# Chunked attention and two gated layers on one core: attention on 64x32 and 64x64 tiles of TensorE

## The chip, the cores and the metric

The kernel runs on one core of a Trainium2 chip. The metric is the device time of one execution in microseconds. A profile shows, for one execution, every instruction of the core's engines: TensorE (PE for its matmuls, PEld for its weight loads), VectorE (DVE), ScalarE (ACT), GpSimd (POOL), and SyncE (SP), which issues the DMA transfers.

## The reference

The program is an attention over chunks, followed by two feed-forward layers on its output. All is in float32.

```python
def _attn_ref(q, k, v, mem_k, mem_v):        # q, k, v: 4 x 8 x 768 x 64, mem: 8 rows
    chunk, left_ctx, right_ctx = (32, 16, 8)
    for c in range(nc):
        k_full = concat(mem_k, k[l_start:r_end]); v_full = concat(mem_v, v[l_start:r_end])
        scores = scale * q_c @ k_full.T
        scores = scores - max(scores, axis=-1)
        a = exp(scores); a = a / (sum(a, axis=-1) + 1e-09)
        out[c_start:c_end] = a @ v_full

def _moe_ref(x, w_in, w_out, alpha):         # 3072 x 512, d_ff = 2048
    h = x @ w_in
    return (maximum(h, 0) + alpha * minimum(h, 0)) @ w_out

def _moe2_ref(x, w_in, w_out):
    h = x @ w_in
    return (h * tanh(softplus(h))) @ w_out

x = attn_out as (3072, 512);  x = _moe_ref(x, ...);  return _moe2_ref(x, ...)
```

Each chunk has 32 queries and sees at most 16 + 32 + 8 keys and 8 memory rows, so 64 keys (the constant SW).

## The kernel before, in words

The weights come as 64-bit words and are turned into float32 on the core (`to_f32`), then split in two parts, high and low (`split_w`), and so are the activations. A product of the feed-forward layers is three matmuls of 128x128 weights and 512 columns (high by high, high by low, low by high): line 694 for the first product of a layer (`gemm1`), line 758 for the second (`gemm2`). They run over 6 blocks of 512 tokens and 16 slices `j` of d_ff, in each of the two layers.

The attention works on 24 tiles of 128 tokens (4 blocks of batch and 6 tiles each). A tile T goes through these steps, and each of the first, third and fourth is a burst on TensorE:

- **scores** (`scores_of`, line 470): 16 matmuls, each with 128 rows of contraction and 64 columns of weights. Two heads share a matmul: the queries stand in a block-diagonal buffer `qbd`, of which half is zeros, so that 128 rows hold two heads of 64.
- **softmax**: on VectorE the maximum (line 485) and, at the end, the division (line 504); on ScalarE eight exponentials with their sums (line 488). Tile 3 takes another way, with one exponential.
- **turn**: the probabilities are transposed, for T < UPT = 5 by TensorE (`turn_pe`, line 580, 16 transposes of 64x96, then copies by `copy_on`, line 250), from then on by VectorE (`turn_dve`, line 606, 8 transposes of 32x256).
- **values** (`values_of`, line 537): 16 matmuls with 96 rows of contraction and 64 columns of weights. The result is split into the halves `xh` (line 554) and `xl` (line 558) of the layers' input.

A matmul of float32 is two passes, so 16 matmuls show 32 records of weight loads (LDWEIGHTS) and 32 of matmuls.

The tiles 0 to 3 (one block of 512 tokens, T < T0) are worked through in front of the layers. While TensorE would wait there, it runs matmuls on a buffer of zeros (`plan.fill`, line 820, called fills below); they stand in its order of work like any other instruction. The tiles 4 to 23 are woven into layer 1: `block_steps` lists the steps, and a step "sv" is one burst with the scores of tile T + 1 and the values of tile T. There are 19 such bursts; beside them stand the scores of tile 4, its transposes, and the values of tile 23, each in a burst of its own.

A planner (`Plan`) sets the order of the instructions on each engine from durations and dependences that the code gives it; the engines then wait on semaphores. PSUM has 8 banks of 512 float32 per partition; in the later part bank 6 takes the scores and bank 7 the values.

Of the kernel before, what the change touches and what calls it, by code (L numbers as in the profile page):

```python
# [174 lines left out]
def chunked_attention_moe_moe_kernel(  # L175
# [37 lines left out]
    UPT = 5  # L213
    BOTH = ("act", "dve")
    WHOLE = (3,)
    T0 = BLOCKS[0][1] // P

# [147 lines left out]
    vring = ring(ac, [W, 2 * DM], F32, "vw", 1)  # L365
# [4 lines left out]
    s_bufs = [own([P, 1024], "s"), spare_slot()]  # L370
    a_bufs = [own([W, 1024], "aT"), spare_slot()]

    def wide_of(b):
        return b.t.rearrange("p (g w) -> p g w", w=P)

    for b in s_bufs:
        for cols in (slice(0, CH), slice(CH + SW, P)):
            add("pool", 0.6, lambda b=b, cols=cols: nc.gpsimd.memset(wide_of(b)[:, :, cols], 0.0), writes=[b])
    for b in qbd:
        for h in range(2):  # L380
            add(
                "pool", 0.6,
                lambda b=b, h=h: nc.gpsimd.memset(
                    b.t.rearrange("p (g h x) -> p g h x", g=2 * NP, h=2)[(1 - h) * 64 : (2 - h) * 64, :, h], 0.0
                ),
                writes=[(b, 2 + h)],
            )
# [4 lines left out]
    att_bufs = [*s_bufs[:1], *a_bufs[:1], *qbd[:2]]  # L392
    n_ps = [0]

    def att_bank(T, late):
        n_ps[0] += 1
        return bank((0, 1, 2, 4, 5, 6, 7)[n_ps[0] % 7] if T < T0 else late)

    def load_qk(T):
        b, t = divmod(T, TPB)  # L400
        kt = kv_spare[T][0] if T in kv_spare else kring.next()
        qt = qbd[T if T < T0 else T % 2]

        def kview():
            return kt.t[:, : NP * KC].rearrange("p (a c) -> p a c", a=NP)

        def qview():
            return qt.t.rearrange("p (a e h x) -> p a e h x", a=NP, e=2, h=2)

        add("sp", dma_(P * NP * KC * 4), lambda: nc.sync.dma_start(kview(), kw[b, t]), writes=[kt])  # L410
        if T < T0:

            row = q_rows[T // 2], T % 2

            def rows():
                return row[0].t[:, row[1] * 512 : (row[1] + 1) * 512]

            add("sp", dma_(P * 2048), lambda: nc.sync.dma_start(rows(), q[b, t].rearrange("h d a e x -> (h d) (a e x)")), writes=[row])
            for h in range(2):

                def place(eng, h=h):
                    half = slice(h * 64, (h + 1) * 64)
                    copy_on(eng, qview()[half, :, :, h], rows()[half].rearrange("p (a e x) -> p a e x", a=NP, e=2))

                add(BOTH if T == 0 else "dve", 0.55, place if T == 0 else partial(place, "dve"), [row], [(qt, h)])
        else:
            for h in range(2):
                add(
                    "sp", dma_(P * 2048),
                    lambda h=h: nc.sync.dma_start(qview()[h * 64 : (h + 1) * 64, :, :, h], q[b, t, h]),  # L430
                    writes=[(qt, h)],
                )
        kts[T], qs[T] = (kt, kview), (qt, qview)
        att_bufs.append(kt)

    def load_v(T):
# [3 lines left out]
        def view():  # L440
            return v.t[:W].rearrange("w (e x) -> w e x", e=2)
# [3 lines left out]
        vws[T] = v, lambda: v.t[:W].rearrange("w (e h d) -> w e h d", e=2, h=H)  # L445
        att_bufs.append(v)

    def scores_of(T):

        t = T % TPB  # L450
        (kt, kview), (qt, qview) = kts[T], qs[T]
        bk = att_bank(T, 6)
        sb = s_bufs[T % 2 if T < T0 else 0]

        def s():
            return wide_of(sb)[:, :, CH : CH + SW]

        st = stats.next()
        ss[T] = sb

        def ps():
            return bk.t.rearrange("p (g c) -> p g c", c=SW)


        def go():
            for e in range(2):
                for p in range(NP):
                    for c in range(2):
                        k0 = e * (U + NM) + c * CH
                        nc.tensor.matmul(  # L470
                            ps()[c * 64 : (c + 1) * 64, e * NP + p, :],
                            qview()[:, p, e].rearrange("p h (x c) -> p (h x) c", c=2)[:, :, c],
                            kview()[:, p, k0 : k0 + SW],
                            start=True, stop=True,
                        )


        def clip():
            if t == 0:
                nc.vector.memset(ps()[0:64, 0:NP, 0:16], NEG)  # L480
            if t == TPB - 1:
                nc.vector.memset(ps()[64:128, NP:, SW - 8 :], NEG)

        def top():
            nc.vector.tensor_reduce(st.t[:, 0, :], ps(), AX.X, ALU.max, negate=True)

        def exps(g):
            nc.scalar.activation(
                s()[:, g, :], ps()[:, g, :], AF.Exp, bias=st.t[:, 0, g : g + 1], scale=0.125,
# [4 lines left out]
        def less():  # L494
            nc.vector.tensor_add(s(), ps(), st.t[:, 0, :].unsqueeze(2).broadcast_to([P, 2 * NP, SW]))  # L495

        def exp():
            nc.scalar.activation(s(), s(), AF.Exp, scale=0.125)
# [7 lines left out]
        def rest():  # L506
            if t in (0, TPB - 1):
                add("dve", 0.15, clip, [], [bk])
            add("dve", d_(512), top, [bk], [(st, 0)])
            if T in WHOLE:  # L510
                add("dve", d_(512), less, [(st, 0), bk], [sb])
                add("act", a_(512), exp, [], [sb])
                add("dve", d_(512), total, [sb], [(st, 1)])
            else:
                add("dve", 0.12, lambda: nc.vector.tensor_scalar_mul(st.t[:, 0, :], st.t[:, 0, :], 0.125), [], [(st, 0)])
                for g in range(2 * NP):
                    add("act", 0.29, lambda g=g: exps(g), [(st, 0), bk], [(sb, g), (st, 1, g)])
# [5 lines left out]
        return go, [kt, qt], [bk], rest  # L523

    def values_of(T):

        (ab, aT), (vb, v) = aTs.pop(T), vws.pop(T)
        bk = att_bank(T, 7)

        def ps():  # L530
            return bk.t.rearrange("p (a e c) -> p a e c", a=NP, e=2)

        def go():
            for e in range(2):
                for p in range(NP):
                    for h in range(2):
                        nc.tensor.matmul(  # L537
                            ps()[h * 64 : (h + 1) * 64, p, e].rearrange("d (c q) -> d c q", c=2),
                            v()[:, e, 2 * p + h, :], aT()[:, e * NP + p, h],
                            start=True, stop=True,  # L540
                        )

        def rest():
# [6 lines left out]
            def flat():  # L550
                return bk.t.rearrange("p (a n) -> p a n", a=NP)

            def high():
                nc.scalar.copy(views()[0][:, :, cols], flat())

            def low():
                xh, xl = (z[:, :, cols] for z in views())
                nc.vector.tensor_sub(xl, flat(), xh.bitcast(F32))
# [381 lines left out]
```

## Time and profile before

| what | us |
|---|---|
| median of 3 runs (1126.13 to 1127.2) | 1126.44 |
| the profiled execution | 1125.74 |
| its span, first to last instruction | 1123.6 |
| TensorE busy (99%) | 1116.2 |
| VectorE busy (71%) | 796.4 |
| ScalarE busy (52%) | 583.3 |

The profiled execution is 0.7 us below the median. A span is cut into stretches below by the start times of instructions; a matmul's record lasts from its issue to its modelled end, so records of matmuls that run behind one another overlap, and it is the distance of their starts that counts. The duration of a pass of 512 columns is 0.39 us, the distance of two of them 0.23 us.

### The profile page before, as it was taken

The page shows a single profiled execution, that of the slowest core. Times are in us where ns is not written, and L with a number is a line of the kernel's source. Part 1 is how long each engine was busy: PE and PEld are TensorE (multiplying, and loading weights), DVE is VectorE, ACT ScalarE, POOL GpSimd, SP SyncE. Part 2 cuts the span into 40 slices and gives each one's busy share as a digit, 9 for nine tenths or more (in the row PEclk, how much of TensorE's full clock was granted, in tenths as well). Part 3 has the DMA queues.
Part 4 walks back from the last instruction along what each step waited for, and adds up shares of the span by engine and source line. Part 5 has one row for each costly group of instructions (what it writes and reads, how often), then busy time and mean ns, then how long its engine had stood idle before and what let it go on. Part 6 is the DMA issues. An engine that isn't in the chain of part 4 may idle for free.

```text
span 1123.6 us, 16499 instructions
## 1 busy us (share of the span) xinstructions
PE 1116.2 (99%) x6286; PEld 920.4 (82%) x6291; DVE 796.4 (71%) x1402; ACT 583.3 (52%) x1268; POOL 6.6 (1%) x20
## 2 busy tenths in 40 slices
PE   8999999999999999999999999999999999999998
PEld 6888888888888888888888888888888888888886
DVE  6899844566556656635449788778878778777775
ACT  6876634454455445445456455445446445444543
POOL 2000000000000000000000000000000000000000
PEclk9999999999999999999999999999999999999999
DMA  9957212264453544334332002002002000100101
GB/s 281 286 172 216 74 37 70 69 181 125 138 157 109 166 124 149 99 104 139 94 101 96 1 1 75 1 1 75 1 1 71 6 1 19 38 1 1 38 1 38
DMA packets 71454, 94.26 MB, mean 84 GB/s; under 512 B 25296, under 2 KB 41680, under 8 KB 71376
## 3 DMA queue, kind: packets, MB, share of 16 engines
q1 hardware_dynamic: 71376, 93.22, 27.8%
q8 instruction: 49, 0.80, 0.3%
q14 instruction: 29, 0.24, 0.1%
HBM read 72.23 MB, written 20.97 MB: 83 GB/s over the span
## 4 chain that ended last, share of the span: by engine, by line
PE 99%; issue 0%; DVE 0%; ACT 0%
PE bank L694 47%; PE bank L758 47%; PE bank L470 2%; PE bank L537 2%; PE bank L820 1%; PE bank L580 0%; DVE wo L495 0%; ACT o L250 0%; DVE busy L818 0%; DVE wi L250 0%
## 5 line engine op out<-in xcount | busy, mean ns | idle before, releaser
L694 PE MATMUL bank<-xh,wi 128*128 128x512 f32 (+1 forms) x1552 | 507.0, 388 | 0.0
L694 PEld LDWEIGHTS bank<-xh,wi 128*128 128x128 f32 x1552 | 290.5, 188 | 60.4 <-DVE wi L332 0.2
L694 PE MATMUL bank<-xl,wi 128*128 128x512 f32 (+1 forms) x776 | 300.2, 387 | 0.0
L758 PE MATMUL bank<-gh,wo 128*128 128x512 f32 x768 | 253.3, 391 | 0.0
L758 PE MATMUL bank<-wo,gh 128*128 128x512 f32 x768 | 236.4, 389 | 0.0
L694 PEld LDWEIGHTS bank<-xl,wi 128*128 128x128 f32 x776 | 145.6, 188 | 29.2
L758 PEld LDWEIGHTS bank<-gh,wo 128*128 128x128 f32 x768 | 144.1, 188 | 30.6 <-DVE rstrip L250 0.3
L758 PEld LDWEIGHTS bank<-wo,gh 128*128 128x128 f32 x768 | 144.2, 188 | 29.9
L716 DVE SCALAR_TENSOR_TENSOR rstrip<-rstrip,nalpha 128x512 f32<-128x512 f32 x96 | 72.0, 750 | 113.8 <-ACT rstrip L713 113.2
L758 PE MATMUL bank<-gl,wo 128*128 128x512 f32 x384 | 149.4, 389 | 0.0
L758 PE MATMUL bank<-wo,gl 128*128 128x512 f32 x384 | 149.4, 389 | 0.0
L706 ACT CAST gh<-u 128x512 fp32r<-128x512 f32 x96 | 59.9, 624 | 156.4 <-PE bank L758 156.3
L712 ACT ACTIVATE rstrip<-bank 128x512 f32<-128x512 f32 x96 | 57.8, 602 | 123.2 <-PE bank L694 115.9
L707 DVE TENSOR_TENSOR gl<-rstrip,gh 128x512 fp32r<-128x512 f32 x96 | 66.3, 691 | 64.8 <-ACT gh L706 63.9
L725 ACT ACTIVATE u<-bank 128x512 f32<-128x512 f32 x96 | 57.5, 599 | 93.2 <-PE bank L694 92.5
L706 ACT CAST gh<-rstrip 128x512 fp32r<-128x512 f32 x96 | 60.1, 626 | 79.5 <-PE bank L758 65.5
L730 DVE SCALAR_TENSOR_TENSOR e<-n,rc 128x512 f32<-128x512 f32 x96 | 66.5, 692 | 48.6 <-ACT rc L729 48.6
L707 DVE TENSOR_TENSOR gl<-u,gh 128x512 fp32r<-128x512 f32 x96 | 66.4, 691 | 42.2 <-ACT gh L706 42.2
L758 PEld LDWEIGHTS bank<-wo,gl 128*128 128x128 f32 x384 | 72.0, 188 | 14.9
L758 PEld LDWEIGHTS bank<-gl,wo 128*128 128x128 f32 x384 | 72.1, 188 | 14.7
L728 ACT ACTIVATE e<-n,two 128x512 f32<-128x512 f32 x96 | 69.2, 721 | 4.5 <-DVE n L727 4.4
L731 DVE SCALAR_TENSOR_TENSOR rc<-e,rc 128x512 f32<-128x512 f32 x96 | 66.4, 692 | 3.2
(84 smaller groups left out, 1000.7 us busy)
## 6 DMA issues: line engine op xcount, KB each, us to landing
wi<-in_w_in_dram SPq DMA_DIRECT2D x16, 512.0 KB, 8.8
wo<-in_w_out_dram SPq DMA_DIRECT2D x16, 512.0 KB, 8.3
raw<-in_w_in_dram SPq DMA_DIRECT2D x16, 512.0 KB, 4.4
raw<-in_w_out_dram SPq DMA_DIRECT2D x16, 512.0 KB, 4.0
vw<-in_vw_dram SPq DMA_DIRECT2D x21, 384.0 KB, 3.7
kt<-in_kw_dram SPq DMA_DIRECT2D x21, 336.0 KB, 4.6
yd<-rstrip SPq DMA_DIRECT2D x24, 256.0 KB, 2.3
raw<-yd SPq DMA_DIRECT2D x24, 256.0 KB, 2.7
```

The source lines that it names most:

```text
L470: nc.tensor.matmul(ps()[c * 64 : (c + 1) * 64, e * NP + p, :], qview()[:, p, e].rearrange("p h (x c) -> p (h x) c", c=2)[:, :, c], kview() ...
L537: nc.tensor.matmul(ps()[h * 64 : (h + 1) * 64, p, e].rearrange("d (c q) -> d c q", c=2), v()[:, e, 2 * p + h, :], aT()[:, e * NP + p, h], ...
L694: nc.tensor.matmul(bk.t[:, lo:hi], a, b, start=kk == 0 and i == 0, stop=kk == KT - 1 and i == 2)
L706: add("act", a_(n), lambda: nc.scalar.copy(g.t[0], src.t[0]), [src], [(g, "h")])
L707: add("dve", d_(n), lambda: nc.vector.tensor_sub(g.t[1], src.t[0], g.t[0].bitcast(F32)), [src, (g, "h")], [(g, "l")])
L712: add("act", a_(n) - 0.05, lambda: nc.scalar.activation(m.t[0], h.t[:, :n], AF.Relu, scale=-1.0), [h], [m])
L716: lambda: nc.vector.scalar_tensor_tensor(r.t[0], m.t[0], nalpha[:, j : j + 1], r.t[0], ALU.mult, ALU.add),
L725: add("act", a_(BN) - 0.05, lambda: nc.scalar.activation(u.t, hs(), AF.Exp), [h], [u])
L728: add("act", a_(BN) + 0.09, lambda: nc.scalar.activation(e.t, n.t, AF.Ln, bias=two[:, 0:1]), [n], [e])
L730: add("dve", d_(BN), lambda: v.scalar_tensor_tensor(e.t, n.t, 2.0, r.t, ALU.add, ALU.mult), [n, r], [e])
L731: add("dve", d_(BN), lambda: v.scalar_tensor_tensor(r.t, e.t, 2.0, r.t, ALU.subtract, ALU.mult), [e], [r])
L758: nc.tensor.matmul(bk.t[:, :n], lt, rh, start=j == 0 and i == 0, stop=j == NJ - 1 and i == 2)
```

## The change

- **Scores**: 32 matmuls in place of 16, each with 64 rows of contraction (one head) and 32 columns of weights (the queries of one chunk). Eight of them, on two groups of rows and four groups of columns, make a round on 64x32 tiles. The queries are used as they were loaded; the block-diagonal buffers, their clearing by GpSimd and the copies into them are gone.
- **Values**: 32 matmuls in place of 16, each with 64 rows of contraction (the keys of one chunk), 64 columns of weights and 32 columns streamed, on 64x64 tiles. Four make a round. The values are loaded per chunk (64 rows, two loads of 256 KB for a tile in place of one of 384 KB).
- **Transposes on TensorE**: 4 of 128x128 for a tile in place of 16 of 64x96, and for T < UPT = 7 in place of 5. The copy behind is one of 512 columns in place of two. VectorE's transposes, for the other tiles, are 16 of 32x128 in place of 8 of 32x256.
- **Banks**: each of banks 6 and 7 holds half of a tile's scores and half of the values; the maximum and the split of the result are two instructions of half the size each.
- The numbers that the planner is given for these bursts are others, so the order of the instructions changes.

```diff
-    UPT = 5
+    UPT = 7
+    HB = BN // 2
...
-    qbd = [own([P, 1024], f"qbd{i}") for i in range(2)] + [spare_slot() for _ in range(2, T0)]
+    q_own = [own([P, 512], f"q{i}") for i in range(2)]
...
-        src = vw[b, 2 * t : 2 * t + 2].rearrange("e w h d -> w e (h d)")
-        add("sp", dma_(W * 4096), lambda: nc.sync.dma_start(view(), src), writes=[v])
+        for e in range(2):
+            rows = vw[b, 2 * t + e].rearrange("w h d -> w (h d)")
+            seen = bass.AP(rows.tensor, rows.offset, [[DM, SW], [CH * DM, 2], [1, DM]])
+            add(
+                "sp", dma_(64 * 4096),
...
+    def open_pair(T):
+        pair["banks"], pair["st"] = [att_bank(T, 6 + z) for z in range(2)], None
...
             for e in range(2):
-                for p in range(NP):
-                    for c in range(2):
-                        k0 = e * (U + NM) + c * CH
-                        nc.tensor.matmul(
-                            ps()[c * 64 : (c + 1) * 64, e * NP + p, :],
-                            qview()[:, p, e].rearrange("p h (x c) -> p (h x) c", c=2)[:, :, c],
-                            kview()[:, p, k0 : k0 + SW],
-                            start=True, stop=True,
-                        )
+                for a in range(NP // 2):
+                    for z in range(2):
+                        for c in range(2):
+                            for h in range(2):
+                                half, row = slice(h * 64, (h + 1) * 64), c * 64 + (h ^ z) * CH
+                                k0 = e * (U + NM) + c * CH
+                                nc.tensor.matmul(
+                                    ps(z)[row : row + CH, 2 * a + e, :],
+                                    qview()[half, 2 * a + z, e].rearrange("p (x c) -> p x c", c=2)[:, :, c],
+                                    kview()[half, 2 * a + z, k0 : k0 + SW],
+                                    start=True, stop=True,
+                                )
...
-            for e in range(2):
-                for p in range(NP):
-                    for h in range(2):
-                        nc.tensor.matmul(
-                            ps()[h * 64 : (h + 1) * 64, p, e].rearrange("d (c q) -> d c q", c=2),
-                            v()[:, e, 2 * p + h, :], aT()[:, e * NP + p, h],
-                            start=True, stop=True,
-                        )
+            for p in range(NP):
+                for c in range(2):
+                    for e in range(2):
+                        for h in range(2):
+                            half = slice(e * 64, (e + 1) * 64)
+                            nc.tensor.matmul(
+                                ps(e)[h * 64 : (h + 1) * 64, p, c],
+                                v()[half, c, 2 * p + h, :],
+                                aT()[half, (p % 2) * (NP // 2) + p // 2, c, h ^ (p % 2)],
+                                start=True, stop=True,
+                            )
...
+        if T < UPT:
+            bk = att_bank(T, 6)
+
+            def turn():
+                for p in range(NP):
+                    cols = slice(p * P, (p + 1) * P)
+                    nc.tensor.transpose(bk.t[:, cols], sb.t[:, cols], ident)
```

In TensorE's order of instructions, the first step "sv" (scores of tile 5, values of tile 4) stood like this between the last product of line 758 and the next of line 694; bank_876 holds scores, bank_893 values, and x16 is a row for 16 instructions:

```order
L758 MATMUL bank_607<-gh,wo_798 128x512
L470 MATMUL bank_876<-kt_730,qbd_101 64x64 x16
L537 MATMUL bank_893<-aT,vw_715 64x64 x16
```

The change has at the same place (its lines are 455 for scores and 525 for values, 741 and 677 for the layers' products; bank_921 and bank_926 are banks 6 and 7, and the pattern of the last rows goes on to 32 matmuls):

```order
L741 MATMUL bank_699<-gh,wo_847 128x512
L455 MATMUL bank_921<-kt_823,q_860 32x64 x4
L455 MATMUL bank_926<-kt_823,q_860 32x64 x4
L455 MATMUL bank_921<-kt_823,q_860 32x64 x4
L455 MATMUL bank_926<-kt_823,q_860 32x64 x4
L455 MATMUL bank_921<-kt_823,q_860 32x64 x4
L455 MATMUL bank_926<-kt_823,q_860 32x64 x4
L455 MATMUL bank_921<-kt_823,q_860 32x64 x4
L455 MATMUL bank_926<-kt_823,q_860 32x64 x4
L525 MATMUL bank_921<-aT,vw_839 64x32 x2
L525 MATMUL bank_926<-aT,vw_839 64x32 x2
```

The burst has 64 instructions in place of 32, in two shapes of tile in place of one, and still stands between the same kinds of products.

In front of the layers, from the transposes of tile 0 on, TensorE's order was this before (line 820 is a fill, with its load of weights as a row of its own):

```order
L580 MATMUL bank_233<-ident,s 96x64 x8
L580 MATMUL bank_245<-ident,s 96x64 x8
L470 MATMUL bank_258<-wo_178,wi_144 64x64 x16
L537 MATMUL bank_282<-aT,vw_211 64x64 x16
L580 MATMUL bank_307<-ident,wo_111 96x64 x8
L580 MATMUL bank_317<-ident,wo_111 96x64 x8
L820 LDWEIGHTS busy
L820 MATMUL bank_87<-busy 128x512
```

In the change the transposes (line 573) and the fills (line 803) stand there so, followed by the scores of tile 3:

```order
L573 MATMUL bank_260<-ident,s 128x128 x4
L803 LDWEIGHTS busy
L803 MATMUL bank_85<-busy 128x512
L803 LDWEIGHTS busy
L803 MATMUL bank_85<-busy 128x512
L803 LDWEIGHTS busy
L803 MATMUL bank_85<-busy 128x512
L803 LDWEIGHTS busy
L803 MATMUL bank_85<-busy 128x512
L455 MATMUL bank_281<-wo_185,wi_145 32x64 x4
```

Where bursts followed one another at once there are fills between them now: from the first instruction to the first product of layer 1, the order has 67 fills in place of 41.

## Rows read from the trace of the kernel before

**Rows 1.** The page: busy us, share of the span, instructions; granted clock in tenths.

```profile
PE 1116.2 (99%) x6286; PEld 920.4 (82%) x6291; DVE 796.4 (71%) x1402; ACT 583.3 (52%) x1268; POOL 6.6 (1%) x20
PEclk9999999999999999999999999999999999999999
```

**Rows 2.** The page: the chain that ended last, shares of the span by line.

```profile
PE bank L694 47%; PE bank L758 47%; PE bank L470 2%; PE bank L537 2%; PE bank L820 1%; PE bank L580 0%; DVE wo L495 0%; ACT o L250 0%; DVE busy L818 0%; DVE wi L250 0%
```

**Rows 3.** The chain in order of time: start us, us, what.

```profile
44.93 2.72 PE bank L694 x12
```

**Rows 4.** TensorE in order of time, one "sv" burst: start us, us, instructions.

```profile
61.94 0.39 PE L758 MATMUL bank<-gh,wo 128*128 128x512 f32 x1
62.26 1.18 PE L470 MATMUL bank<-kt,qbd 128*64 128x64 f32 x32
63.27 1.10 PE L537 MATMUL bank<-aT,vw 96*64 96x64 f32 x32
64.30 0.50 PE L694 MATMUL bank<-xh,wi 128*128 128x512 f32 x1
```

**Rows 5.** The weight loads of that burst in order of time, with idle time before.

```profile
62.26 1.04 PEld L470 LDWEIGHTS bank<-kt,qbd 128*64 128x64 f32 x32 [0.35 <-issue]
63.21 1.01 PEld L537 LDWEIGHTS bank<-aT,vw 96*64 96x64 f32 x32
```

**Rows 6.** Line 470 in two stretches: us, busy us (records) of PE and PEld.

```profile
62.25:62.27 0.02, 0.01 (x2) 0.01 (x2) 1.00 0.00 0
62.26:63.21 0.95, 0.95 (x31) 0.95 (x32) 1.00 0.00 0
```

**Rows 7.** Line 537 in its stretch of the burst, the same columns.

```profile
63.21:64.15 0.94, 0.88 (x32) 0.94 (x32) 1.00 0.00 0
```

**Rows 8.** Lines 470, 580: durations ns (min/median/max), first and last start.

```profile
L470 PE MATMUL bank<-kt,qbd x672: 222/223/273, 5.5 to 458.2; 128*64 128x64 f32 x168
L580 PE MATMUL bank<-ident,s x48: 216/216/257, 13.2 to 51.0; 64*96 64x64 f32 x48
```

**Rows 9.** Line 537's waits on its sequencer: durations ns, first and last start.

```profile
L537 PEldq EVENT_SEMAPHORE  x24: 51/51/51, 14.4 to 474.4; - x24
```

**Rows 10.** TensorE in order of time: tile 4's scores, tile 4's transposes.

```profile
37.74 0.39 PE L758 MATMUL bank<-gh,wo 128*128 128x512 f32 x1
38.06 1.19 PE L470 MATMUL bank<-kt,qbd 128*64 128x64 f32 x32
39.18 0.50 PE L694 MATMUL bank<-xh,wi 128*128 128x512 f32 x1
...
49.98 0.39 PE L758 MATMUL bank<-gh,wo 128*128 128x512 f32 x1
50.30 0.92 PE L580 MATMUL bank<-ident,s 64*96 64x64 f32 x16
51.15 0.50 PE L694 MATMUL bank<-xh,wi 128*128 128x512 f32 x1
```

**Rows 11.** TensorE in order of time, in front of the layers.

```profile
9.04 1.67 PE L820 MATMUL bank<-busy 128*128 128x512 bf16 x7 [0.16 <-issue]
...
14.02 1.18 PE L470 MATMUL bank<-wo,wi 128*64 128x64 f32 x32
15.03 1.10 PE L537 MATMUL bank<-aT,vw 96*64 96x64 f32 x32
...
18.05 1.02 PE L820 MATMUL bank<-busy 128*128 128x512 bf16 x4 [1.06 <-DVE wo L495]
...
24.84 0.47 PE L694 MATMUL bank<-xh,wi 128*128 128x256 f32 x1
```

**Rows 12.** Stretches: us, busy us (records) PE, PEld, DVE, ACT, POOL; clock; DMA.

```profile
32.30:120.00 87.70, 87.70 (x640) 72.15 (x640) 82.24 (x165) 68.23 (x185) 0.00 (x0) 1.00 0.70 200
```

**Rows 13.** Line 606, VectorE's transposes: durations ns.

```profile
L606 DVE STREAM_TRANSPOSE aT<-s x152: 424/434/443, 71.0 to 471.9; 32x256 f32<-32x256 f32 x152
```

**Rows 14.** The page: DMA's busy share in tenths, 40 slices.

```profile
DMA  9957212264453544334332002002002000100101
```

More of the change, by code (lines that the diff above doesn't have):

```diff
@@ L401, in load_qk, with flat @@
         kt = kv_spare[T][0] if T in kv_spare else kring.next()
-        qt = qbd[T if T < T0 else T % 2]
+        if T < T0:
+            buf, off = q_rows[T // 2], T % 2 * 512
+            qt = buf, T % 2
+        else:
+            buf, off = q_own[T % 2], 0
+            qt = buf
+        def flat():
+            return buf.t[:, off : off + 512]
         def kview():
@@ L407, in qview @@
         def qview():
-            return qt.t.rearrange("p (a e h x) -> p a e h x", a=NP, e=2, h=2)
+            return flat().rearrange("p (a e x) -> p a e x", a=NP, e=2)
         add("sp", dma_(P * NP * KC * 4), lambda: nc.sync.dma_start(kview(), kw[b, t]), writes=[kt])
[L411 to L431, printed above, removed]
-                )
+        add("sp", dma_(P * 2048), lambda: nc.sync.dma_start(flat(), q[b, t].rearrange("h d a e x -> (h d) (a e x)")), writes=[qt])
         kts[T], qs[T] = (kt, kview), (qt, qview)
@@ L497, in exp @@
         def exp():
[L498 removed]
+            nc.scalar.activation(sb.t[:, :512], sb.t[:, :512], AF.Exp, scale=0.125)
         def total():
@@ L506, in rest @@
         def rest():
-            if t in (0, TPB - 1):
-                add("dve", 0.15, clip, [], [bk])
-            add("dve", d_(512), top, [bk], [(st, 0)])
+            for z in range(2):
+                if t in (0, TPB - 1):
+                    add("dve", 0.15, partial(clip, z), [], [(bks[z], "s")])
+                add("dve", d_(HB), partial(top, z), [(bks[z], "s")], [(st, 0, z)])
             if T in WHOLE:
-                add("dve", d_(512), less, [(st, 0), bk], [sb])
+                for z in range(2):
+                    add("dve", d_(HB), partial(less, z), [(st, 0), (bks[z], "s")], [(sb, z)])
                 add("act", a_(512), exp, [], [sb])
@@ L569, in aT, with turn_of @@
+            for e in range(2):
+                done = [(st, 1, g) for g in range(e * NP, (e + 1) * NP)] if st else []
+                add("act", a_(HB), partial(high, e), [(bks[e], "v")] + done, [(x, ("h", T), e)])
+                add("dve", d_(HB), partial(low, e), [(bks[e], "v"), (x, ("h", T), e)], [(x, ("l", T), e)])
+        return go, [ab, vb], [(b, "v") for b in bks], rest
+    def turn_of(T):
+        sb, ab = ss.pop(T), a_bufs[T % 2 if T < T0 else 0]
         def aT():
-            return ab.t[:W].rearrange("k (g h c q) -> k g h c q", g=2 * NP, h=2, c=2)
+            return ab.t[:, :512].rearrange("k (p c h q) -> k p c h q", p=NP, c=2, h=2)
@@ L572, in turn_pe @@
         aTs[T] = ab, aT
-        for c in range(2):
-            bk = att_bank(T, 6 + c)
-            def turn(bk=bk, c=c):
-                rows = slice(c * 64, (c + 1) * 64)
-                k0 = (1 - c) * CH
-                for g in range(2 * NP):
-                    nc.tensor.transpose(
-                        bk.t[0:W, g * 64 : (g + 1) * 64], wide_of(sb)[rows, g, k0 : k0 + W], ident[rows, rows]
-                    )
-            def back(eng, bk=bk, c=c):
-                copy_on(eng, aT()[:, :, :, c, :], bk.t[0:W].rearrange("k (g h q) -> k g h q", g=2 * NP, h=2))
-            add("pe", 0.47, turn, [sb] + behind(T), [bk])
-            add(BOTH if T < T0 else "act", a_(512), back if T < T0 else partial(back, "act"), [bk], [(ab, c)])
@@ L610, in new_x, with turn @@
+        for i in range(4):
+            for j in range(4):
+                def turn(i=i, j=j):
+                    src = sb.t[i * CH : (i + 1) * CH, :512].rearrange("p (a k) -> p a k", k=P)
+                    nc.vector.transpose(aT()[j * CH : (j + 1) * CH, :, i // 2, i % 2], src[:, :, j * CH : (j + 1) * CH])
+                add("dve", 0.26, turn, [sb], [(ab, (i, j))])
     def new_x(n):
```

127 lines of the change are left out of this document (53 added, 74 removed).

## The prediction

> **What bounds the kernel now.** I read the page first: TensorE is busy for 1116.2 of the span's 1123.6 us, at the full granted clock in every slice [rows 1]. The chain that ended last is TensorE's almost alone: 47% and 47% for the layers' products, 2% each for scores and values [rows 2]. So time is won only by taking work off TensorE, and only where its stream is dense. Twelve products follow one another in 2.72 us, 0.227 each [rows 3]; that is the yardstick for what a burst of attention costs on top.
>
> Then I read one burst "sv" in order of time [rows 4]. The last product before it starts at 61.94, the next is issued at 64.30. That one lasts 0.50 instead of 0.39 because its weights are not loaded yet, so it really runs from 64.41. The burst costs 64.41 - 61.94 - 0.23 = 2.24 us, and 19 of them 42.6. The single burst of scores costs 39.29 - 37.74 - 0.23 = 1.32, tile 4's transposes 51.26 - 49.98 - 0.23 = 1.05 [rows 10].
>
> **Inside a burst.** Scores take 0.95 us for 32 passes [rows 6], values 0.94 for 32 [rows 7]. In the first 20 ns two loads and two matmuls of line 470 are under way [rows 6]: two column groups already run side by side. So there are 16 rounds of two passes, 59 ns each. The rest of the 2.24, 0.35, is way in and out: about 0.14 from the last product to the first pass, 0.2 at the end. The loads show it as 0.35 without work before line 470 and none before line 537, which has the same shape of tile [rows 5].
>
> What makes a round 59 ns? The first matmul of a burst waits for its own load, and lasts 273 instead of 223 ns [rows 8]: the load of 128 rows by 64 columns takes 50. Streaming has to be worked out: a product's record of 0.39 less the 0.21 to 0.23 that its 512 columns take leaves 0.16 to 0.18 of passage, and a pass of 223 ns less that leaves 45 to 60 for its 64 columns. Both limits lie together, and half of either alone shortens nothing.
>
> **Scores, after.** A round is eight passes on 64x32 tiles, so 64 passes are 8 rounds. Streaming is unchanged (64 columns), so a round stays near 58: 0.46 us in place of 0.95. What the trace does not show is eight tiles at once; it shows two.
>
> **Values, after.** A round is four passes: 16 rounds as before. Streaming is halved to 32 columns, about 27 ns. The load is 64 rows by 64 columns. The nearest row with 64 rows is the transposes': 96 columns load in 257 - 216 = 41 ns [rows 8], which makes 27 for 64. By the other row, line 470's (64 columns, but 128 rows), it stays 50. With 27 a round is some 33 ns and values take 0.53; with 50 it is 58 and they take 0.93. I take the row with the same 64 rows, and keep the other for the range.
>
> **A switch inside the burst.** Scores and values now have different tiles. The row on the way in says what a change of tile costs: 0.14 [rows 4, 5]. I add 0.15. [...]
>
> A burst "sv" becomes 0.14 + 0.46 + 0.15 + 0.53 + 0.2 = 1.48, which is 0.76 less: 19 x 0.76 = **-14.5 us**. Scores of tile 4: 0.14 + 0.46 + 0.2 = 0.80, **-0.5**. Values of tile 23: 0.87 in place of 1.27 (0.14 + 0.93 + 0.2), **-0.4**.
>
> **Transposes in the stream.** Now one tile (1.05), after three (tiles 4 to 6). Sixteen of 64 identity columns take 0.85 us [rows 10], 53 ns each; four of 128 columns are 0.43, with 0 to 0.35 for way in and out, as a 128x128 tile is the products' own shape. I take 0.6: 3 x 0.6 - 1.05 = **+0.75** (bounds +0.2 and +1.3).
>
> **In front of the layers.** TensorE executes its order there, fills included. The order has 67 fills ahead of the first product in place of 41: 26 x 0.215 = +5.6 us, with (1.67 - 0.38) / 6 = 0.215 from one series [rows 11]. Scores save 4 x 0.49, values 4 x 0.40, transposes (0.92 to about 0.55) 4 x 0.35: -5.0. An idle of 1.06 and one of 0.16 before fills should close [rows 11]: -1.2. Sum **-0.6**. With slow values it is +1.0; a late transfer may add to it, as the value loads grow by 128 KB a tile while DMA is at 9 tenths and more in the first two slices [rows 14]. From +2 to -2 covers this.
>
> **Costed at nothing.** VectorE loses the transposes of tiles 5 and 6 (2 x 8 x 0.434 = 6.9 us [rows 13]) in the stretch where it is busiest, 82.2 of 87.7 us [rows 12]; for tiles 7 and 8 sixteen at between half and all of 0.434 add 0 to 3.5 each. So its cover there doesn't shrink. The halved maxima, casts and subtractions lie beside products on the other engines; if that cover were gone, some 0.4 us a tile would show. Copies into block-diagonal buffers and GpSimd's clearing vanish, from the front only, where the fills decide. If tile 5 or 6 comes late to its transposes, TensorE stalls there, for a microsecond at most, with the products of line 694 queued behind.
>
> **Sum**: -14.5 - 0.5 - 0.4 + 0.75 - 0.6 = -15.3. Against its own execution, 1125.74 - 15.3 = 1110.4 (span about 1108); the median stands 0.7 higher, so 1111.
>
> **Rivals.**
>
> *Loads of values don't get cheaper.* The values' round stays at 58 ns. "sv" is then 0.14 + 0.46 + 0.15 + 0.93 + 0.2 = 1.88, which saves 0.36 x 19 = 6.8; with -0.5, 0, +0.75 and +1.0 the sum is -5.6, or 1121. For it speaks line 470's 50 ns for 64 columns [rows 8]; against it the transposes' 41 for 96. [...] Chance 0.22.
>
> *Instructions are handed over too slowly* (the slower side). The change has 64 float32 matmuls per burst in place of 32. If each takes as long to reach the array as one takes now, 0.95 / 16 = 59 ns, tiles stand empty however many there are. The burst is 64 x 59 + 0.35 = 4.1, +1.9 x 19 = +36; tile 4 and tile 23 add 1.9, the front 5.6 of fills and 8 x 0.95 of bursts less 1.4 of transposes and 1.2 of idle, +10.6, the late transposes 0.75: about 1175. It decides from about 28 ns an instruction, where 64 of them fill today's 1.9 us less the switch. Against it: a wait of line 537, which stands behind sixteen matmuls of scores in the order, is executed at 14.4 [rows 9], 0.4 us after those scores begin at 14.02 and 0.6 before the values start at 15.03 [rows 11]. That is at most 27 ns each if all came after 14.02, and more if some had been handed over before. Nothing shows a faster rate. [...] Half the overlap would give half of the 14.5, about 1118, which lies inside the range. Chance 0.10 for slower.
>
> *The gain is eaten*: the bursts get shorter, but slow values meet a dear switch (0.35 in place of 0.15, +3.8), and front and late transposes stand at their upper bounds (+2, +1.3): -6.8 - 0.5 + 7.1, about 1126. Chance 0.04.
>
> **Numbers.** The forecast has 0.64. Its own range is 1103 to 1115: below, if the switch costs nothing (-2.9), rounds stand at 50 and 27 ns rather than 58 and 33 (-3), and the front gives 2 (-1.4); above, if the front stands at +2 and each switch costs 0.08 more. Slow values reach 1123 with the front's upper bound. I give 1103 to 1122. A measurement of this kernel tells 0.2% (2.3 us) from no change. Faster: 0.64 + 0.22 = 0.86; same 0.04; slower 0.10.
>
> **What would show it.** The chain must stay TensorE's. In order of time a burst must have 64 records of scores, starting eight in 60 ns, over in about half a microsecond; then a gap without loads; then values four by four, in about 0.5 us (right) or 0.9 (first rival). Distance from the last product before to the next one behind: 1.7 us (2.47 now). If the records' starts are evenly spaced at 15 ns or more in both parts, the hand-over is the limit. The late transposes must cost 0.4 to 0.8 each, and the first product of layer 1 start near 24.2. The prediction is wrong if a wait of TensorE for VectorE or ScalarE of more than a microsecond appears in blocks 0 to 4, or if line 741's products get longer.

## The result, and the profile after

The changed kernel takes 1132.31 us (median of 4 runs, 1130.55 to 1133.3), the kernel before 1126.45: a ratio of 1.0052 (95% interval 1.0039 to 1.0065). It is slower by 5.9 us, where 15.4 us less were predicted (1111). The profiled execution took 1132.87 us, its span is 1131.1 (1123.6 before).

The page after, where it answers to [rows 1, 2]: busy us, share and instructions; granted clock in tenths; a DMA queue with packets, MB and share; the chain by line.

```profile
PE 1118.4 (99%) x7792; PEld 918.0 (81%) x7800; DVE 812.9 (72%) x1576; ACT 579.1 (51%) x1284; POOL 1.0 (0%) x8
PEclk9999999999999999999999999999999999999999
q8 instruction: 61, 1.00, 0.4%
PE bank L677 47%; PE bank L741 46%; PE bank L525 2%; PE bank L455 2%; PE bank L803 1%; ACT s L472 0%; PE bank L573 0%; ACT wo L472 0%; DVE st L469 0%; ACT o L251 0%; DVE busy L801 0%; DVE st L502 0%; DVE bank L464 0%; ACTq L472 0%
```

The bound is the same engine, with 1506 more pairs of weight load and matmul (7792 for 6286). The tenths of the clock show nothing; only narrower stretches will. New line numbers: scores 470 is now 455, values 537 is 525, TensorE's transposes 580 are 573, VectorE's 606 are 587, fills 820 are 803, the layers' products 694 and 758 are 677 and 741.

First the steady part, which the prediction was about. One "sv" burst and one late transpose in TensorE's order of time (start us, us, instructions), as [rows 4, 10]:

```profile
59.26 0.39 PE L677 MATMUL bank<-xh,wi 128*128 128x512 f32 x1
59.49 0.60 PE L573 MATMUL bank<-ident,s 128*128 128x128 f32 x4
59.84 0.48 PE L741 MATMUL bank<-gh,wo 128*128 128x512 f32 x1
...
67.89 0.39 PE L741 MATMUL bank<-gh,wo 128*128 128x512 f32 x1
68.21 0.86 PE L455 MATMUL bank<-kt,q 64*32 64x64 f32 x64
69.00 1.13 PE L525 MATMUL bank<-aT,vw 64*64 64x32 f32 x64
70.07 0.50 PE L677 MATMUL bank<-xh,wi 128*128 128x512 f32 x1
...
11.46 0.81 PE L803 MATMUL bank<-busy 128*128 128x512 bf16 x3 [0.16 <-issue]
12.11 0.49 PE L573 MATMUL bank<-ident,s 128*128 128x128 f32 x3
14.16 0.27 PE L573 MATMUL bank<-ident,s 128*128 128x128 f32 x1 [1.56 <-ACT s L472]
...
19.80 0.77 PE L525 MATMUL bank<-aT,vw 64*64 64x32 f32 x36
23.09 0.65 PE L525 MATMUL bank<-aT,vw 64*64 64x32 f32 x28 [2.52 <-issue]
...
31.89 1.00 PE L525 MATMUL bank<-aT,wi 64*64 64x32 f32 x51 [0.51 <-issue]
...
35.98 0.40 PE L677 MATMUL bank<-xh,wi 128*128 128x256 f32 x2
38.37 0.58 PE L677 MATMUL bank<-xl,wi 128*128 128x256 f32 x1 [1.98 <-issue]
...
47.39 0.58 PE L741 MATMUL bank<-gh,wo 128*128 128x512 f32 x1
```

The burst runs from 67.89 to 70.07 + 0.11, so it costs 70.18 - 67.89 - 0.23 = 2.06 us over the yardstick, in place of 2.25; 19 of them 39.1 in place of 42.7. The transpose costs 59.84 + 0.09 - 59.26 - 0.23 = 0.44. So later blocks won some 4 us.

The rest of the rows is the front, and there 12.1 us went: the first product of layer 1's second half starts at 47.39; in the kernel before it started at 35.25:

```profile
35.25 0.39 PE L758 MATMUL bank<-gh,wo 128*128 128x512 f32 x1
```

Four times TensorE stands still there. Three times the profile names no releaser ("issue"), and the stop falls into the middle of a burst (36 passes of values, then 2.52 us of nothing, then the other 28), where no semaphore is due. Why that is, the next views show. Pairs of load and matmul between the stops (stretch, PE, PEld, DVE, ACT, POOL busy us with records, clock, DMA share, GB/s), and three stretches behind stops:

```profile
0.00:12.60 12.60, 10.78 (x218) 5.55 (x222) 4.13 (x15) 5.97 (x34) 0.98 (x8) 1.00 0.88 266
12.60:20.50 7.90, 6.18 (x125) 3.91 (x126) 5.66 (x15) 4.23 (x21) 0.00 (x0) 1.00 1.10 217
20.50:31.40 10.90, 8.05 (x129) 4.40 (x126) 4.32 (x11) 3.39 (x8) 0.00 (x0) 0.84 1.06 308
31.40:36.30 4.90, 4.25 (x127) 3.45 (x128) 1.59 (x4) 1.20 (x5) 0.00 (x0) 1.00 1.08 378
...
23.90:28.50 4.60, 4.59 (x16) 1.91 (x15) 3.44 (x8) 1.53 (x4) 0.00 (x0) 0.63 1.08 334
33.00:38.37 5.37, 3.33 (x77) 2.45 (x76) 2.63 (x6) 1.84 (x6) 0.00 (x0) 0.95 1.06 374
38.37:47.50 9.13, 9.13 (x54) 8.46 (x55) 4.62 (x8) 5.22 (x10) 0.00 (x0) 0.85 0.14 53
```

From stop to stop it is 126 to 129 pairs each time. The page's queue q8 carries 61 packets for 7800 pairs, 128 pairs a packet (49 packets for 6291 pairs in the kernel before, 128 again). So the stops stand at the ends of blocks that TensorE's own instructions are fetched in, 16 KB each (1.00 MB in 61). The DMA queues in two stretches of the changed kernel, from the first stop's place to the second, and during the second stop (packets, MB, share of 16 engines):

```profile
q1 hardware_dynamic: 1142, 1.65, 109.3%
...
q1 hardware_dynamic: 170, 0.31, 100.1%
q8 instruction: 1, 0.02, 5.8%
```

In 12.6 to 20.3 us no packet of instructions is under way, and the data take all 16 DMA engines; the one packet starts at 20.32, 6.2 us after TensorE had gone into the block before (14.16). It ends at 21.62, and TensorE goes on at 23.09. At the other two it is the same: packets from 29.45 to 30.55 and from 35.89 to 36.98, and TensorE goes on at 31.89 and 38.37, 1.3 to 1.5 us behind them. When the data have thinned out, a packet starts about 1 us behind the block's start (39.43 for 38.37). And behind two of the stops the clock is granted at half for a while, at 0.50 from 24.13 to 27.54 us and from 37.78 to 41.19: the mean is 0.63 and 0.85 in the first and the last of the three stretches. In the stretch between (0.95) it falls while TensorE stands still, from 37.8 us on.

### The profile page after: what moved, and what is told of

Read it like the earlier page. It is cut to its first block, busy times and chain, and to the rows that moved or that the text cites. A ratio compares the mean times of both kernels' runs of the same rounds, so it can differ in the third digit from the quotient of the medians.

```text
span 1131.1 us, 19694 instructions
## 1 busy us (share of the span) xinstructions
PE 1118.4 (99%) x7792; PEld 918.0 (81%) x7800; DVE 812.9 (72%) x1576; ACT 579.1 (51%) x1284; POOL 1.0 (0%) x8
## 4 chain that ended last, share of the span: by engine, by line
PE 98%; ACT 1%; issue 1%; DVE 0%; ACTq 0%
PE bank L677 47%; PE bank L741 46%; PE bank L525 2%; PE bank L455 2%; PE bank L803 1%; ACT s L472 0%; PE bank L573 0%; ACT wo L472 0%; DVE st L469 0%; ACT o L251 0%; DVE busy L801 0%; DVE st L502 0%; DVE bank L464 0%; ACTq L472 0%
## 5 line engine op out<-in xcount | busy, mean ns | idle before, releaser
L587 DVE STREAM_TRANSPOSE aT<-s 32x128 f32<-32x128 f32 x272 | 82.2, 302 | 4.6
L472 ACT ACTIVATE s<-bank,st 128x64 f32<-128x64 f32 x176 | 53.0, 323 | 39.7 <-DVE st L502 39.5
```

The lines of the kernel that those rows point to most:

```text
L472: nc.scalar.activation(s()[:, g, :], ps(g // NP)[:, g % NP, :], AF.Exp, bias=st.t[:, 0, g : g + 1], scale=0.125, accum_out=st.t[:, 1, g : ...
L587: nc.vector.transpose(aT()[j * CH : (j + 1) * CH, :, i // 2, i % 2], src[:, :, j * CH : (j + 1) * CH])
```

## The experiments

The theory before the first runs: in the front, where the data fill the DMA queues, a fetch of 128 pairs takes some 8 us (an estimate from the 8.9, 8.8 and 6.5 us from one stop's end to the next), and the change doubles the pairs of scores and values, so TensorE runs dry. Rivals: the larger and later value loads; 26 more fills; transposes that wait for ScalarE (the row at 14.16). In the runs below, times of other chips are compared by their ratios to the kernel before; the changed kernel's own is 1.0052.

**1. More pairs alone, in the kernel before.**

```diff
-    matmul(idle.t, busy[:, :P], busy)                                  # a fill
+    [matmul(idle.t[:, i*P:(i+1)*P], busy[:, :P], busy[:, i*P:(i+1)*P]) for i in range(4)]
```

> The kernel before, with each of its fills (one matmul of 512 bf16 columns) issued as four of 128 columns: the same columns and the same transfers, but 123 more pairs of weight load and matmul ahead of the layers (about as many as the change adds there). Theory (the front of the changed kernel is lost to fetches of TensorE's own instructions, which wait their turn among the data transfers): a fetch comes every 128 pairs, so blocks are used up sooner, and TensorE stops once or twice in the front for 0.5 to 2.5 us with nothing to wait for ('issue'), at lower clock behind it; 2 to 8 us slower, near 1131. Rivals (later and larger value loads, more fills in the order, transposes that wait for ScalarE): none of these is in this kernel, so within 1 us of 1126.4, no stop over 0.5 us.

1131.18 us, ratio 1.0040 (1.0025 to 1.0055): 4.7 us slower, as the theory says. The waits of TensorE in this kernel (line, releaser: us, times, longest), two rows of its order of time, and the stretch between the stops:

```profile
PE bank L470 <- issue: 1.7, 1, 1.7
PE bank L537 <- issue: 1.0, 1, 1.0
...
15.96 1.75 PE L470 MATMUL bank<-wo,wi 128*64 128x64 f32 x32 [1.70 <-issue]
23.62 0.39 PE L537 MATMUL bank<-wi,wi 96*64 96x64 f32 x5 [1.02 <-issue]
...
14.20:22.50 8.30, 6.60 (x129) 6.20 (x127) 3.66 (x9) 5.58 (x22) 0.00 (x0) 0.79 1.08 290
```

The stops come behind the 229th and the 358th pair (places in TensorE's order, with the waits between the pairs counted in), where two of the changed kernel's come, though it is other work that stands there, and the clock falls behind the first (0.79 in the last row).

**2. The same pairs, thinner transfers.** Ten early weight loads of layer 1 and their splits are left out of the changed kernel.

```diff
+    def light(item): return item[0] == 0 and (2 if item[1] == "i" else 0) <= item[2] < 6
+            if light(item): return          # no load, no split; input weights 0 or 1 stand in
```

> The changed kernel without ten of the layer's early weight loads and their splits (output weights 0 to 5, input weights 2 to 5; two loaded ones are used in their place, so the output is not the reference's): TensorE's instructions and their order are the same, but the transfers are less dense from 18 us on. Theory of late fetches: the stops for issue at 20.4, 31.4 and 36.4 us shrink to under 0.5 us together or vanish, the clock stays at full, the first product of line 741's kind begins near 38 to 40 us instead of 47.3, and the time is 7 to 10 us shorter, 1122 to 1125. Rival (26 more fills, and transposes that wait for ScalarE): these stay, so the front shortens by 2 us at most.

1128.01 us, ratio 1.0013 (1.0004 to 1.0022), 4.4 us less than the changed kernel; in the profiled executions 5.5 us. The product that started at 47.39 starts at 41.38. One row is left of the three stops for issue:

```profile
PE bank L587 <- ACT s L486: 1.8, 1, 1.8
PE bank L539 <- issue: 1.0, 1, 1.0
```

Those at 31.4 and 36.4 us are gone, that at pair 358 has shrunk to 1.0 (its packet still started at 20.26, among the data). Less came back than the 7 to 10 us expected. The data fill the queues until about 26 us (the share of the 16 engines is 1.04 from 22 to 24 us, 0.93 to 26 and 0.10 to 28), so the stops behind the pairs 228 and 358 are still there, and so are all the fills. With the loads, the work of ten splits on VectorE and ScalarE is left out too. This run alone does not separate the two; the profile of the changed kernel names neither engine at the two stops that are gone.

**3. Later loads or more fills?** Two versions of the changed kernel.

```diff
-    not_before=at if layer else 0.0                # after_vfirst
+    not_before=at if layer else 14.2 if j < 2 else 0.0
-    plan.fill = lambda t: 0.44 if t < 6.8 else 0.22    # after_fills
+    plan.fill = lambda t: 0.44
```

> The changed kernel with the first two weight loads held in the planner until the value loads of tiles 0 and 1 are out, the order that they had in the kernel before; values of tile 0 then stand ahead of tile 2's transposes again. If the front was lost because values come later, 5 us or more come back (1127 or less). If it was lost to late fetches of instructions, the same pairs stand there and the transfers are as dense: the stops for issue stay at the ends of the blocks of 128 pairs, and 0 to 3 us come back.

> The changed kernel with the planner's price of a fill at 0.44 throughout, so that 41 fills stand ahead of the layers as in the kernel before, in place of 67. If the 26 fills were the loss, 26 x 0.215 = 5.6 us come back (1126.7). If the stops for instructions set the front, TensorE waits at the same ends of blocks instead, with more idle time before them, and 0 to 3 us come back.

1130.00 us (1.0037, 1.0023 to 1.0051) and 1130.60 (1.0040, 1.0024 to 1.0055). That is no more than experiment 5's first version shows (1.0040), which changes nothing in the front. A row of the waits of the first:

```profile
PE bank L525 <- issue: 4.0, 1, 4.0
```

and two rows of TensorE in order of time, and one stretch, of the second:

```profile
13.99 0.91 PE L455 MATMUL bank<-wo,wi 64*32 64x64 f32 x61 [1.32 <-issue]
...
23.34 0.65 PE L525 MATMUL bank<-aT,vw 64*64 64x32 f32 x14 [4.15 <-issue]
...
22.60:36.24 13.64, 12.56 (x195) 8.29 (x196) 5.76 (x13) 4.03 (x10) 0.00 (x0) 0.50 1.07 353
```

Both stand still behind pair 358, now for 4.0 and 4.15 us in place of 2.52. In the second, TensorE's waits sum to nearly the same as in the changed kernel (8.6 for 9.1 us), but the clock stays at 0.50 from 22.6 to 36.2 us, which costs half of 12.56, 6.3 us, in place of 3.1. That leaves 5.6 - 3.2 = 2.4 us of what the fills took; the first product of line 741's kind does start 2.3 us earlier, at 45.11. So fewer fills are a gain that the clock takes back in good part, and the fills are not cleared as a part of the loss.

The first of these rows settles the transposes: it is the place of the changed kernel's row at 14.16, 228 pairs from the start, but with fewer fills scores stand there and the releaser is "issue". The wait "for ScalarE" was the first of the four stops, under a name that the profile inferred: in all eight versions with the changed bursts in front, it stands behind the same 228 pairs; in the changed kernel that is 1.6 us behind the end of a packet (12.57).

**4. The old front, the new rest.** Tiles 0 to 3 by the code before, with its loads, its fills and its order on TensorE; from tile 4 on the changed code. Then the same with 128 KB more loaded per tile, with fewer fills, and with none behind the sixth microsecond.

```diff
+    def scores_of(T): return (scores_of_old if T < T0 else scores_of_new)(T)    # also load_qk, load_v, values_of, turn_of
+    nc.sync.dma_start(v.t[W:P], src[: P - W])       # hybrid_load: rows that nobody reads
+    plan.fill = lambda t: 0.44                      # hybrid_fills
+    plan.fill = lambda t: 0.44 if t < 6.8 else 99.0 # hybrid_nofills
```

> The kernel before for tiles 0 to 3 (block-diagonal queries, 96-key values, its transposes, its loads and its fills, in the same order on TensorE), the changed one from tile 4 on. If all that was lost was lost in the front, and the rest gained as the two traces say (19 bursts at 2.06 in place of 2.25 us, tile 4's scores 0.99 in place of 1.32, three late transposes of 0.45 in place of one of 1.05), the first product of line 758's kind begins at 35.3 as before, and the time is 1126.5 - 3.6 - 0.3 + 0.3 = 1122.9, 1122 to 1124. If the later blocks lose something too, it stays within 1 us of 1126.5.

1120.40 us, ratio 0.9950 (0.9937 to 0.9962), which makes 1120.8 beside 1126.45, 2.1 us better than expected. The steady part is the changed kernel's (19 bursts at 2.06 us, transposes at 0.44), and the front is that of before. Of the 5.0 us between the two spans, 3.6 are the bursts and 0.7 lie behind the last product (4.1 us to the end in place of 4.8), where nothing was tried. TensorE in order of time, three rows of the front:

```profile
17.70 1.24 PE L1023 MATMUL bank<-busy 128*128 128x512 bf16 x5 [1.13 <-issue]
...
34.90 0.39 PE L897 MATMUL bank<-xh,wi 128*128 128x512 f32 x1
35.12 0.39 PE L961 MATMUL bank<-gh,wo 128*128 128x512 f32 x1
```

The first row is the counterpart of the 1.06 at 18.05 in [rows 11], which that profile puts down to VectorE. Here, with the same order on TensorE, it is "issue", behind the 230th pair: the kernel before had one such stop already.

> The version with the old front (1120.4 us), with 128 KB more loaded for each of tiles 0 to 3, as the change loads them (rows that nobody reads), and priced so in the planner. If the larger value loads by themselves cost the front, some 4 x 0.6 us at the 217 GB/s of that stretch, 2 us or more are lost (1122.5 or above). If what cost the front is the number of pairs between the fetches, which stays as it is, at most 1 us is lost.

1121.07 us, ratio 0.9955 (0.9942 to 0.9969): 0.6 us lost, inside both intervals. The larger loads by themselves are not the loss. The executions reach from 1119.81 to 1123.33; the profiled one is the longest, and the stop behind pair 230 takes 1.7 us in it.

> The version with the old front, with a fill priced at 0.44 throughout, so that about half of the fills behind the sixth microsecond fall away. If the fetch that comes late at pair 230 (TensorE stood still from 16.6 to 17.7 us) sets the front, the same pair is only reached sooner and waits longer: within 1 us of 1120.4. If fills are time that nothing needs, 1 to 3 us are won (1117.5 to 1119.5).

1118.75 us, ratio 0.9932 (0.9920 to 0.9945), the fastest version here, 2.0 us less by the ratios: as the second expectation had it. The same product starts at 33.56, 1.56 us earlier. Some of the fills were time that nothing needed. Near pair 230 a stop of 0.55 us is left, until 17.84; the profile puts it down to a copy on ScalarE, which ends just before, at 17.79.

> The version with the old front and no fill at all behind the sixth microsecond (11 of 41 are left), so TensorE stands still wherever its next work is late. Halving the fills gave 1.65 us, by which the first product of line 758's kind came 1.56 us earlier. If the rest of them is not needed either, another 0 to 1 us is won (1118 to 1118.8). If the idle time lowers the granted clock in the front, as the stops of the changed kernel did, products or bursts run at half clock and 1 to 4 us are lost (1120 to 1123).

1124.75 us, ratio 0.9984 (0.9973 to 0.9995): 3.8 us lost against the version with all fills. The executions reach from 1121.71 to 1127.17, with a mean clock from 0.997 to 0.989; the profiled one took 1126.59. Its stretches, same columns as above:

```profile
0.00:12.00 12.00, 8.50 (x109) 4.74 (x109) 5.18 (x15) 5.36 (x26) 6.47 (x20) 1.00 0.84 262
12.00:20.00 8.00, 6.85 (x100) 6.41 (x102) 4.58 (x12) 6.24 (x31) 0.00 (x0) 0.50 1.10 249
20.00:28.00 8.00, 7.21 (x98) 6.58 (x97) 7.14 (x16) 5.56 (x11) 0.00 (x0) 0.50 1.06 353
28.00:38.00 10.00, 10.00 (x78) 9.66 (x78) 5.07 (x9) 4.64 (x10) 0.00 (x0) 0.61 0.85 299
```

From 12 to 28 us the clock is at 0.50; with half of the fills it was 1.00 in the same stretches.

**5. What sets a round of values?** Three versions of the changed kernel, for tiles 4 to 23: 32 columns streamed twice in each pass; the two row halves one after the other; each pass preceded by one that loads 33 columns.

```diff
-    aT()[half, idx, c, hh]                                              # after_cols64
+    aT()[half, idx, c, hh].unsqueeze(1).broadcast_to([64, 2, CH])
-    for p in range(NP): for c in range(2): for e in range(2): ...       # after_rows
+    for e in range(2): for p in range(NP): for c in range(2): ...
+    for m in (33, 64): matmul(ps(e)[h*64 : h*64+m, p, c], v()[half, c, 2*p+h, :m], ...)   # after_load33
```

> The changed kernel with the values of tiles 4 to 23 streaming their 32 columns twice (64 columns per pass; the second half is overwritten by the next pass), loads as they are. If load and streaming of a tile follow one another (28 + 30 ns make today's 58), a round becomes about 85 ns, values 1.36 us in place of 0.93, and the time grows by 20 x 0.42 = 8.4 us. If a pass on a tile has a floor of 58 ns whatever it streams, or loads are hidden behind streaming as in the kernel before, the round stays at 58 and the time within 1 us of 1132.3.

> The changed kernel with the values of tiles 4 to 23 in another order: first all passes on rows 0 to 63 (two tiles), then all on rows 64 to 127, so two tiles are at work instead of four. If each tile takes 58 ns per pass whatever the others do, the 32 rounds take 1.86 us in place of 0.93: 18 us slower. If load and streaming overlap as they did on two tiles in the kernel before, and four tiles at once are what keeps them apart, a round is about 30 ns and values stay near 0.95: within 1 us of 1132.3.

> The changed kernel with each pass of values of tiles 4 to 23 preceded by one on the same tile that loads only 33 of the 64 columns (its result is overwritten): 16 more rounds per burst. If a tile has a floor of 58 ns per pass, whatever is loaded and streamed up to 64 columns, these rounds cost 58 ns too: 20 x 0.93 = 18.6 us, near 1151. If load and streaming add up, they cost 28 x 33/64 + 30 = 44 ns: 14.2 us, near 1146.5. Hand-over at 17 ns an instruction would be 32 x 17 = 0.54 us a burst, 11 us, if the tiles were free.

1131.42 us (1.0040, 1.0026 to 1.0054), 1147.58 (1.0185, 1.0169 to 1.0200) and 1166.32 (1.0361, 1.0338 to 1.0384). A burst's values in order of time, in the first, in the second, and two bursts of the third:

```profile
69.94 1.14 PE L527 MATMUL bank<-aT,vw 64*64 64x64 f32 x64
```

```profile
67.93 1.86 PE L526 MATMUL bank<-aT,vw 64*64 64x32 f32 x64
```

```profile
67.38 1.47 PE L526 MATMUL bank<-aT,vw 64*33 64x32 f32 x112
70.46 0.38 PE L526 MATMUL bank<-aT,vw 64*33 64x32 f32 x16 [1.61 <-issue]
...
399.56 1.66 PE L526 MATMUL bank<-aT,vw 64*33 64x32 f32 x128
```

Twice the streamed columns change nothing (1.14 for 1.13), two tiles in place of four take the time again (1.86, and 20 x 0.73 = 14.6 us of the 15 measured; it is less than the 0.93 expected, and that passes of the two halves overlap where one follows the other is the author's estimate). So each tile has its own pace, and streaming, of 32 columns or 64, does not set it. The third tells what does: 64 more passes cost 1.66 - 1.13 = 0.53 us, 33 ns a round; none of the three expectations had that mechanism (the last had nearly its size: 32 matmuls handed over at 17 ns each are 0.54 us). In the records the distance of two starts on one tile is 58 ns behind a pass with 64 loaded columns and 32 to 33 behind one with 33, from the start of the burst to its end. Four rounds with their eight matmuls take 182 ns, 23 a matmul, so the hand-over has time to run ahead and is not needed to explain the 33; that it plays a part in the rounds of 33 no run excludes. For these passes the pace goes by the loaded columns, 0.9 to 1.0 ns each. The contraction hardly shows in it: 58 ns for 64 columns on 64 rows, 59 on 96 and on 128 [rows 6, 7]. It is not the pace of every kind of pass: the transposes of the kernel before load 96 columns and follow one another at 53 ns on the mean [rows 10].

Of the third's loss, 20 x 0.53 = 10.6 us are these rounds. The rest is the theory of the front over again, with fewer data under way (0.60 of the 16 engines from 69 to 92 us): a burst of 192 pairs runs through more than one block, and the row at 70.46 stands still in it. Eleven stops in values sum to 17.3 us, two of them in the front, and the mean clock is 0.991 (0.997 in the changed kernel).

**6. VectorE's cover.** The changed kernel with tiles 5 and 6 transposed on VectorE, as before.

```diff
-    UPT = 7
+    UPT = 5
```

> The changed kernel with tiles 5 and 6 transposed on VectorE again, in sixteen pieces each: TensorE sheds 2 x 0.45 us in the stream, VectorE takes up 2 x 16 pieces of about 0.3 us. If VectorE has room there, 0.9 us shorter (1131.4); if it has none, TensorE waits for it in block 1 and the time grows by 1 us or more.

1144.32 us, ratio 1.0166 (1.0150 to 1.0182): 13 us slower than the changed kernel. A row of the waits, its stretches, and the durations (ns min/median/max) of line 587:

```profile
PE bank L525 <- DVE aT L587: 4.8, 9, 1.0
...
100.00:120.00 20.00, 17.32 (x180) 13.80 (x180) 17.14 (x45) 12.88 (x38) 0.00 (x0) 0.83 0.46 146
120.00:140.00 20.00, 18.31 (x124) 14.93 (x125) 18.79 (x42) 11.17 (x34) 0.00 (x0) 0.91 0.20 57
...
L587 DVE STREAM_TRANSPOSE aT<-s x304: 289/303/309, 81.1 to 490.2; 32x128 f32<-32x128 f32 x152
```

Sixteen pieces of 0.303 us are 4.8 us a tile, where eight of 0.434 were 3.5 [rows 13]. TensorE waits 4.8 us for them in the middle of bursts, and the clock falls behind the waits, 20 x 0.17 + 20 x 0.09 = 5.2 us. The profiled execution (1142.65 us, the shortest) is 9.8 us longer than the changed kernel's, and these are 10; but its front is 2.0 us shorter (the first product of line 741's kind starts at 45.39) and TensorE sheds two transposes, so some 3 us are not accounted for. With sixteen pieces a tile VectorE has no room there, between 86 and 123 us, unless TensorE turns tiles 5 and 6.

## Why the prediction was wrong

**In front of the layers** (-0.6, measured +12.1) is the step that failed. It took every fill and every burst for its own duration, and its only reserve was a late transfer of data, +2 at most. That instructions are transfers as well, and that more pairs use up a block of them sooner, it did not see. The pieces: the fills +5.6 as said; bursts -2.2 in place of -5.0 (scores 0.86 for 1.18 in three tiles of four, transposes 0.60 for 0.92 in all four; values no shorter); four stops of 1.7, 2.6, 0.6 and 2.2, where before had one of 0.8, by the distances of starts, +6.3; half clock behind them, by the stretches shown 4.6 x 0.37 + 9.1 x 0.15 = 3.1. That is +12.8; the pieces overlap, since fills also pass time in which a stop would be longer and keep the clock up (experiment 3: 0.50 from 22.6 to 36.2 us with 41 of them). The idle of 1.06 that "should close" was itself the first stop. It was named after VectorE, and the prediction took the name at its word.

**Values** (0.53 for 0.93). The choice between two rows was wrong: it took the one with the same 64 rows, the transposes', which are another kind of pass, and the right one was line 470's with its 64 columns. The first rival, with a chance of 0.22, had it: the round stayed at 58 ns. That is 19 x 0.40 = 7.6 us of the missing gain, and tile 23's values saved nothing.

**Scores** (0.46). The mechanism was right: eight tiles do run at once, 32 passes in 0.24 us. From the 33rd on a new matmul of two passes starts only every 17 ns, and all 64 take 0.65. This is the second rival's mechanism at 17 ns an instruction in place of 59; it costs 19 x 0.19 = 3.6 us. That the hand-over is the limit is read from the starts alone; no run changed it.

**The switch** (0.15) and the ways in and out (0.14, 0.2) held in sum: 0.14 + 0.65 + 0.15 + 0.93 + 0.2 = 2.07, measured 2.06 (0.09 on the way in, 0.25 on the way out). So "sv" gave -3.6 in place of -14.5.

**Scores of tile 4**: -0.33 for -0.5, for the same reason. **Transposes in the stream**: 3 x 0.44 - 1.05 = +0.27 for +0.75; four records of 109 ns, and nothing for way in and out, the lower bound.

**Costed at nothing**: right for the later blocks; no wait of TensorE shows there, and experiment 6 tells that moving tiles 5 and 6 was needed for it.

**Sum**: -3.6 - 0.3 + 0.3 + 12.1 = +8.5; the span grew by 7.5, with 0.8 less behind the last product. Without the front's loss the gain is what experiment 4 shows, 5.6 us by the ratio: about 1121, and not 1111. That is the first rival's time, but not by its sum, which had 6.8 us for "sv" where 3.6 were measured, and lost 1.0 in front; the 0.7 us behind the last product, which no term had, make up for some of it.

## What to carry to other kernels

Count instructions as transfers. Where many small matmuls meet a stretch in which data fill the DMA queues, compare the pairs per microsecond with what a fetch brings (here 128 pairs in 6.5 to 9 us among the data; with free queues 1.1 + 1.0 + 1.4 = some 3.5 us, an estimate from the packet at 39.43). A stop labelled "issue", or one that stands a block of 128 pairs from the next whatever the label says, is a sign of it. Fills are not only lost time: with fewer of them the clock stayed low for longer (experiments 3 and 4), and in the old front half of them could go. More tiles at once helped here only as far as the loaded columns shrank and the instructions arrived: 64x32 tiles gained on scores (0.65 us for 0.95), 64x64 tiles with half the streamed columns gained nothing on values (0.93 for 0.94).

## What the runs showed of the hardware

- TensorE's instructions came in packets of 16 KB for 128 pairs of load and matmul. In the changed kernel a packet started 4.0 to 6.4 us behind the start of the block before it while data filled the queues, about 1 us when they did not. In the fronts of the two kernels it took 1.0 to 1.4 us, and behind a stop TensorE went on 1.3 to 1.7 us after its end.
- Behind the stops of 2.5 and 2.0 us the granted clock fell, to a mean of 0.63 over 4.6 us and 0.85 over 9.1, which cost 3.1 us more. In the old front with only 11 fills it stood at 0.50 from 12 to 28 us, in the changed front with 41 fills from 22.6 to 36.2 us.
- The pace of the passes of values on one tile went by the loaded columns: 58 ns for 64, with 32 or 64 columns streamed, and 32 to 33 for 33, with 32 streamed. The transposes of the kernel before do not follow it (53 ns with 96 loaded columns).
- Open: why a packet takes its turn so late among the data, and whether fewer outstanding loads would help it. Neither was tried.
